# One group of 65536 keys a head in a decode attention kernel: scores in SBUF, one maximum, values in 32 KB rows

## The chip, the core and the metric

The kernel runs on one core of one Trainium2 chip. The core has a matrix engine (TensorE, PE in the profile), a vector engine (VectorE, DVE), a scalar engine (ScalarE, ACT), a general engine (GpSimd, POOL) and a synchronising engine (SyncE, SP), each with its own instruction queue that is worked through in order. Sixteen DMA engines move data from the chip's memory (HBM) to the on-chip memory SBUF, which has 128 partitions. PE writes its results to a second on-chip memory, PSUM. The metric is the device time of one execution in microseconds (us); lower is better.

## The reference

One token of a decoder, with two branches that are added:

```python
xn = _layernorm(x)
return x + _A_ref(xn, A_k_cache, A_v_cache, A_wq, A_wo) + _B_ref(xn, B_w1, B_w2, B_w3, B_w4)

def _A_ref(x, k_cache, v_cache, wq, wo):        # Hq = 32, Hkv = 4, Sk = 65536, Dh = 128, D = 1024
    q = (x @ wq) as [1, 32, 1, 128]
    k = repeat(k_cache, 8 times along the heads); v likewise
    scores = einsum("bhqd,bhkd->bhqk", q, k) * 128 ** -0.5
    p = softmax(scores)
    o = einsum("bhqk,bhkd->bhqd", p, v)
    return o as [1, 1, 4096] @ wo

def _B_ref(x, w1, w2, w3, w4):                  # one position: the shifts of the reference leave zeros here
    h = gelu(layernorm(x) @ w1); hs = concat(shifted parts of h) @ w2; x1 = x + hs
    return x1 + gelu(layernorm(x1) @ w3) @ w4
```

Everything is in bfloat16. Four key-value heads serve 8 query heads each. K and V are 67 MB each, the six weight matrices together some 36 MB: 170 MB are read once. A softmax needs the largest score before its exponentials (or a correction afterwards, when a larger one turns up).

## The kernel before, in words

The program is written with explicit queues. Every operation is appended to the list of its engine by a helper (`_op`, `_grp` for a group, `_dma`), which also adds waits on the semaphores of what it reads and overwrites. The order of the Python code is thus the order in each engine's queue.

**Slots and loads.** All large inputs pass through eight slots of SBUF, `slots_sb`, each of 16 KB a partition (8192 elements of 2 bytes). `load` (L290) fills one slot with 2 MB, `load2` (L296) two neighbouring slots with 4 MB in one transfer, and then needs an even slot number (`room`, L278). Slots are taken in a ring. All these transfers are issued on SP's queue. Lists `loads` and `uses` (L608 on) hold the order; after each use the function `issue` (L636) hands out as many further loads as have slots in the order of the list. On SP, a load waits until what was in its slots has been read. `wq` (8 MB, for the queries), `w1`, `w2` and `w3` come first, `w4` last, and a 2 MB part of `wo` a head in between.

**Groups.** The keys of a head are cut in two groups of 32768. A group has four chunks of 8192 keys (`NCH = 4`, 64 keys a partition). K of a group comes as two transfers of 4 MB: a partition's 256 keys of the group are 64 KB in HBM, of which each transfer takes 32 KB. V comes as four transfers of 2 MB, one a chunk, 16 KB a partition and without gaps. Chunks of K of group g alternate with chunks of V of group g-1.

**Scores.** `use_k` (L515) turns one chunk: four 32x32 block transposes by DVE (L522, 128x1024 in f32 units) from the slot to one of two buffers `X`, then 16 matrix products by PE (L529) into one of four PSUM banks `S_ps`, one bank a chunk, then DVE's maximum of the bank (L534). Eight query heads and sixteen key positions share the 128 PSUM partitions.

**Maximum and exponentials.** After four chunks `finish_group` (L536) takes the maximum over the chunks, brings it together over the partitions of a query head by one product (L543) and a minimum of the negated values, and updates a running maximum `brun` (L545 to L548). ACT then computes four exponentials from PSUM to `p_sb` with their sums (L553), and a correction factor `ff` for the second group (L557).

**Values.** `transpose_p` (L559) runs behind the first K chunk of the next group: eight PE transposes (L562) into PSUM and an ACT copy to `pT_sb` (L565), twice. `use_v` (L569) does 16 products a chunk (L575), summed in one PSUM bank `OT_ps`. `flash` (L580) copies the first group's result to `O_acc` (L585, ACT) and rescales and adds the second's (L588, L592, DVE). At a head's end `combine` (L594) sums the parts with five products (L595, L597) and four DVE steps (L600 to L604), which give the head's 1024 outputs for `use_wo`.

Of the kernel before, what the change touches and what calls it, by code (L numbers as in the profile page):

```python
# [133 lines left out]
def bass_parallel_sum__gqa_block_cached__mixer_s_mlp__decode_kernel(  # L134
# [23 lines left out]
    NCH = 4  # L158
    NA = 4
    SUB = P * CR  # L160
    GRP = SUB * NCH
    GPH = SK // GRP
    NG = HKV * GPH
    NK = NG * NCH
# [4 lines left out]
    assert DH == P and G == 8 and HKV == 4 and D == 1024 and HQD == 4096 and F == 3584 and SK % GRP == 0  # L169
# [5 lines left out]
    with ExitStack() as es:  # L175
# [42 lines left out]
        p_sb = sb("p_sb", [P, CL, 32, NCH], BF)  # L218
        pT_sb = sb("pT_sb", [P, 2, NA, CL * 4, G], BF)
        mcol = sb("mcol", [P, 2, NCH], F32)  # L220
        mrow = sb("mrow", [P, 2], F32)
        Rm = sb("Rm", [P, 2, 16], BF)
        Bst = sb("Bst", [P, NG], F32)
        brun = sb("brun", [P, 2], F32)
        dd = sb("dd", [P, 1], F32)
        ff = sb("ff", [P, 1], F32)
        lcol = sb("lcol", [P, 2, NCH], F32)
        lsum = sb("lsum", [P, 1], F32)
# [15 lines left out]

        S_all = ps("S_ps", [P, NCH * 512], F32)
        S_ps = [S_all[:, 512 * i:512 * (i + 1)] for i in range(NCH)]
# [110 lines left out]
        def load_v(g, a):
            h, gb = divmod(g, GPH)
            s0 = gb * GRP + a * SUB
            return load(A_v_cache[0, h, s0:s0 + SUB, :].rearrange("(p c) d -> p (c d)", p=P))  # L360

# [153 lines left out]
        def use_k(g, ch, ld):  # L515
            view, b = ld[0:2]
            n = g * NCH + ch
            h = g // GPH
            m = n % 2
            K32 = view.bitcast(F32)  # L520
            for ix in range(4):
                _op(q_dve, lambda e, ix=ix: e.transpose(out=X32[:, m, 1024 * ix:1024 * (ix + 1)], in_=K32[:, 1024 * ix:1024 * (ix + 1)]),  # L522
                    reads=b, writes=[b_X[m][ix]])
            fns = []
            for we in range(4):
                w_hi, e_ = divmod(we, 2)
# [7 lines left out]
            _op(q_dve, lambda e: e.reduce_max(mcol[:, gm, ch:ch + 1], S_ps[ch][:, :], axis=AX.X), reads=[b_S[ch]], writes=[b_mcol[gm]], partial=ch > 0)  # L534

        def finish_group(g):  # L536
            h, gb = divmod(g, GPH)
            m = g % 2
            kn, ko = gb % 2, (gb - 1) % 2
            _op(q_dve, lambda e: e.reduce_max(mrow[:, m:m + 1], mcol[:, m, :], axis=AX.X), reads=[b_mcol[m]], writes=[b_mrow[m]])  # L540
            _op(q_dve, lambda e: e.tensor_tensor(out=Rm[:, m, :], in0=sel16[:, :], in1=mrow[:, m:m + 1].broadcast_to([P, 16]), op=ALU.mult),
                reads=[b_mrow[m], b_const], writes=[b_R[m]])
            _op(q_pe, lambda e: e.matmul(M0_ps[:, 16:32], Lmat[:, :], Rm[:, m, :], start=True, stop=True), reads=[b_R[m], b_sel], writes=[b_M0])  # L543
            if gb == 0:
                _op(q_dve, lambda e: e.tensor_reduce(out=brun[:, 0:1], in_=M0_ps[:, 16:32], axis=AX.X, op=ALU.min), reads=[b_M0], writes=[b_brun[0]])  # L545
            else:
                _op(q_dve, lambda e: e.tensor_reduce(out=Bst[:, g:g + 1], in_=M0_ps[:, 16:32], axis=AX.X, op=ALU.min), reads=[b_M0], writes=[b_Bst])
                _op(q_dve, lambda e: e.tensor_tensor(out=brun[:, kn:kn + 1], in0=brun[:, ko:ko + 1], in1=Bst[:, g:g + 1], op=ALU.min),  # L548
                    reads=[b_brun[ko], b_Bst], writes=[b_brun[kn]])
                _op(q_dve, lambda e: e.tensor_tensor(out=dd[:, :], in0=brun[:, kn:kn + 1], in1=brun[:, ko:ko + 1], op=ALU.subtract),  # L550
                    reads=[b_brun[ko], b_brun[kn]], writes=[b_dd])
            for ch in range(NCH):
                _op(q_act, lambda e, ch=ch: e.activation(p_sb[:, :, :, ch], S_ps[ch][:, :].rearrange("p (c i) -> p c i", i=32),  # L553
                                                         ACTF.Exp, bias=brun[:, kn:kn + 1], scale=SCALE, accum_out=lcol[:, m, ch:ch + 1]),
                    reads=[b_S[ch], b_brun[kn]], writes=[b_p, b_lcol[m]], partial=ch > 0)
            if gb > 0:
                _op(q_act, lambda e: e.activation(ff[:, :], dd[:, :], ACTF.Exp), reads=[b_dd], writes=[b_ff])  # L557

        def transpose_p(g):  # L559
            m = g % 2  # L560
            for c8 in range(CL // 8):
                _grp(q_pe, [lambda e, i=i, c=8 * c8 + i: e.transpose(out=PT_ps[:, i * P:(i + 1) * P],  # L562
                                                                    in_=p_sb[:, c, :, :].rearrange("p i h -> p (i h)"), identity=ident_bf[:])
                            for i in range(8)], reads=[b_p, b_const], writes=[b_PT])
                _op(q_act, lambda e, c8=c8, m=m: e.activation(pT_sb[:, m, :, 32 * c8:32 * c8 + 32, :].rearrange("p a x g -> p x a g"),  # L565
                                                              PT_ps[:, :].rearrange("p (x a g) -> p x a g", x=32, a=NA), ACTF.Copy),
                    reads=[b_PT], writes=[b_pT[m]], partial=c8 > 0)

        def use_v(g, a, ld):  # L569
            view, b = ld[0:2]  # L570
            m = g % 2
            fns = []
            for cl in range(CL):
                q4 = cl % 4
                fns.append(lambda e, cl=cl, q4=q4: e.matmul(OT_ps[32 * q4:32 * q4 + 32, :], pT_sb[:, m, a, 4 * cl:4 * cl + 4, :].rearrange("p x g -> p (x g)"), view[:, 512 * cl:512 * (cl + 1)],  # L575
                                                            start=(a == 0 and cl < 4), stop=(a == NA - 1 and cl >= CL - 4), tile_position=(0, 32 * q4),
                                                            skip_group_check=True))
            _grp(q_pe, fns, reads=b + [b_pT[m]], writes=[b_OT], partial=a > 0)

        def flash(g):  # L580
            gb = g % GPH
            m = g % 2
            _op(q_dve, lambda e: e.reduce_sum(lsum[:, :], lcol[:, m, :], axis=AX.X), reads=[b_lcol[m]], writes=[b_lsum])
            if gb == 0:
                _op(q_act, lambda e: e.activation(O_acc[:, :], OT_ps[:, :], ACTF.Copy), reads=[b_OT], writes=[b_O])  # L585
                _op(q_dve, lambda e: e.tensor_copy(Lacc[:, :], lsum[:, :]), reads=[b_lsum], writes=[b_Lacc])
                return
            _op(q_dve, lambda e: e.tensor_scalar(out=O_acc[:, :], in0=O_acc[:, :], scalar1=ff[:, 0:1], scalar2=None, op0=ALU.mult),  # L588
                reads=[b_ff], writes=[b_O])
            _op(q_dve, lambda e: e.tensor_scalar(out=Lacc[:, :], in0=Lacc[:, :], scalar1=ff[:, 0:1], scalar2=lsum[:, 0:1], op0=ALU.mult, op1=ALU.add),  # L590
                reads=[b_ff, b_lsum], writes=[b_Lacc])
            _op(q_dve, lambda e: e.tensor_tensor(out=O_acc[:, :], in0=O_acc[:, :], in1=OT_ps[:, :], op=ALU.add), reads=[b_OT], writes=[b_O])  # L592
# [17 lines left out]
        for g in range(NG):  # L610
            for cp in range(2):
                loads.append(("k", g, cp))
                if g > 0:
# [101 lines left out]
```

## Time and profile before

| what | value |
|---|---|
| median of 3 runs | 406.20 us (406.18 to 406.21) |
| the profiled execution | 406.29 us |
| its span, first to last instruction | 404.6 us |
| mean granted TensorE clock | 0.615 |
| HBM read | 169.87 MB, 420 GB/s over the span |
| transposes of K (L522, DVE) | 128 times 1211 ns, 147.7 us |
| score products (L529, PE) | 512, 59.9 us busy |
| exponentials (L553, ACT) | 32 times 1412 ns, 45.2 us |
| value products (L575, PE) | 512, 55.9 us busy |

The page of the profile shows one execution. Busy times are sums over instructions; PE's matrix products overlap, so the busy time is less than count times mean. The rows of 40 slices give each engine's busy share in tenths, the clock that was granted to PE, and the share and rate of the sixteen DMA engines. The table of queues gives a DMA queue's packets, its MB, and the time that its packets took as a share of sixteen engines over the span. The chain of waits goes back from the last instruction to what released it, step by step. Timelines give the start of an instruction (or of a run of equal ones), its length, engine and line. The trace also holds each DMA packet with its start, length and size.

### The profile page before, as it was taken

Reading aid. Unit: us, or ns where it says so; the run is one execution under the profiler, and the core shown is the slowest. Engines: PE = TensorE matmul, PEld = TensorE weight load, DVE = VectorE, ACT = ScalarE, POOL = GpSimd, SP = SyncE. Lnnn points to the kernel's source line nnn. Section 1 sums busy time; section 2 is a strip of 40 time slices with the busy share of each in tenths; the row PEclk is TensorE's granted clock in tenths of the full one; section 3 lists DMA queues with packets and bytes.
Section 4 is the critical chain, followed back from the end, with each engine's and each line's share of the span. In section 5 each row is a group of like instructions: output and inputs, shape, how many; then the busy total and the mean of one; then the engine's idle time right before and its main releaser. Section 6 shows DMA issues by size and latency. Waiting matters only on the chain.

```text
span 404.6 us, 4047 instructions
## 1 busy us (share of the span) xinstructions
PE 170.8 (42%) x1651; PEld 75.4 (19%) x1651; DVE 200.4 (50%) x304; ACT 65.2 (16%) x91; POOL 7.5 (2%) x38
## 2 busy tenths in 40 slices
PE   0273231223555345435335363535252436355626
PEld 0122110102212112211121131212121122122313
DVE  0255027667667665755173737571545655740010
ACT  1000000006007105200610041106010232034000
POOL 5000000000000000000000000000000000000000
PEclk9985655555655965665556655656565657655656
DMA  8999999999999999999999999999999999999995
GB/s 357 421 415 426 452 415 444 413 437 420 462 400 431 429 447 411 441 414 444 411 450 410 437 424 441 415 427 439 423 433 434 423 434 424 420 434 420 444 405 197
DMA packets 9682, 170.13 MB, mean 421 GB/s; under 512 B 1208, under 2 KB 1216, under 8 KB 2112
## 3 DMA queue, kind: packets, MB, share of 16 engines
q1 hardware_dynamic: 9512, 169.88, 98.5%
q8 instruction: 13, 0.21, 0.2%
q14 instruction: 5, 0.04, 0.0%
q10 hardware_dynamic: 152, 0.00, 0.0%
HBM read 169.87 MB, written 0.00 MB: 420 GB/s over the span
## 4 chain that ended last, share of the span: by engine, by line
DMA 57%; DVE 21%; PE 13%; issue 6%; ACT 2%; SPq 0%; POOL 0%; ACTq 0%
DMA slots_sb<-in_A_k_cache_dram 47%; DVE X L522 17%; PE S_ps L529 8%; DMA slots_sb<-in_B_w_dram 7%; DMA xr_bf<-in_A_x_dram 3%; DVE mcol L534 3%; PE OT_ps L575 2%; PE S_ps L440 2%; ACT p_sb L553 1%; ACT pT_sb L565 1%; PE PT_ps L562 1%; PE M_ps L424 0%; PE M_ps L416 0%; PE M_ps L543 0%; SPq L317 0%
## 5 line engine op out<-in xcount | busy, mean ns | idle before, releaser
L522 DVE STREAM_TRANSPOSE X<-slots_sb 128x1024 f32<-128x1024 f32 x128 | 147.7, 1211 | 39.1 <-DMA slots_sb<-in_A_k_cache_dram 39.1
L529 PE MATMUL S_ps<-X,Yall 128*32 128x512 bf16 x512 | 59.9, 614 | 150.4 <-DVE X L522 150.4
L553 ACT ACTIVATE p_sb<-S_ps,brun 128x512 bf16<-128x512 f32 x32 | 45.2, 1412 | 195.5 <-DVE brun L545 105.2
L575 PE MATMUL OT_ps<-slots_sb,pT_sb 128*32 128x512 bf16 x512 | 55.9, 584 | 12.8 <-ACT pT_sb L565 9.6
L534 DVE TENSOR_REDUCE mcol<-S_ps 128x1 f32<-128x512 f32 x32 | 22.1, 692 | 69.2 <-PE S_ps L529 69.2
L529 PEld LDWEIGHTS S_ps<-X,Yall 128*32 128x32 bf16 x512 | 17.3, 126 | 185.8 <-DVE X L522 169.4
L575 PEld LDWEIGHTS OT_ps<-slots_sb,pT_sb 128*32 128x32 bf16 x512 | 18.5, 132 | 37.9 <-issue 32.2
L565 ACT ACTIVATE pT_sb<-PT_ps 128x1024 bf16<-128x1024 bf16 x16 | 16.4, 1023 | 55.6 <-PE PT_ps L562 55.6
L562 PE MATMUL PT_ps<-ident_bf,p_sb 128*128 128x128 bf16 x128 | 15.3, 294 | 11.8 <-ACT pT_sb L565 8.9
L440 PE MATMUL S_ps<-slots_sb,xn_bf 128*32 128x512 bf16 (+1 forms) x128 | 12.6, 567 | 10.7 <-DMA slots_sb<-in_B_w_dram 9.2
L562 PEld LDWEIGHTS PT_ps<-ident_bf,p_sb 128*128 128x128 bf16 x128 | 11.4, 133 | 20.3 <-ACT pT_sb L565 11.0
L592 DVE TENSOR_TENSOR O_acc<-O_acc,OT_ps 128x512 f32<-128x512 f32 x4 | 2.8, 688 | 16.5 <-PE OT_ps L575 16.5
L440 PE MATMUL M_ps<-slots_sb,gh_bf 128*32 128x256 bf16 x112 | 6.5, 399 | 7.7 <-DMA slots_sb<-in_B_w_dram 7.6
L444 DVE STREAM_TRANSPOSE X<-S_ps 128x512 f32<-128x512 f32 (+1 forms) x3 | 2.5, 848 | 14.2 <-PE S_ps L440 14.2
L452 ACT ACTIVATE ge_a<-ge_b 128x8 f32<-128x8 f32 (+1 forms) x2 | 0.4, 217 | 52.2 <-DVE ge_b L451 52.2
L678 DVE TENSOR_TENSOR fin<-accr,M_ps 128x256 bf16<-128x256 f32 x1 | 0.4, 421 | 16.3 <-PE M_ps L440 16.3
L553 ACT ACTIVATION_READ_ACCUMULATOR p_sb<-S_ps,brun 128x1 f32 x32 | 8.5, 264 | 0.0
L440 PE MATMUL M_ps<-slots_sb,oP_bf 128*32 128x256 bf16 x128 | 7.7, 420 | 1.4 <-DVE oP_bf L604 1.4
L597 PE MATMUL M_ps<-O_acc,selX 128*128 128x128 f32 x32 | 8.2, 439 | 0.0
L440 PEld LDWEIGHTS S_ps<-slots_sb,xn_bf 128*32 128x32 bf16 x128 | 4.3, 133 | 17.0 <-DMA slots_sb<-in_B_w_dram 9.9
L597 PEld LDWEIGHTS M_ps<-O_acc,selX 128*128 128x128 f32 x32 | 7.3, 333 | 0.0
L395 DVE CAST xP<-xP_bf 128x8 f32<-128x8 bf16 x1 | 0.2, 172 | 14.2 <-DMA xr_bf<-in_A_x_dram 14.2
(97 smaller groups left out, 70.1 us busy)
## 6 DMA issues: line engine op xcount, KB each, us to landing
slots_sb<-in_A_k_cache_dram SPq DMA_DIRECT2D x16, 4096.0 KB, 26.9
slots_sb<-in_A_v_cache_dram SPq DMA_DIRECT2D x32, 2048.0 KB, 30.7
slots_sb<-in_A_wq_dram SPq DMA_DIRECT2D x2, 4096.0 KB, 16.8
slots_sb<-in_A_wo_dram SPq DMA_DIRECT2D x4, 2048.0 KB, 27.5
slots_sb<-in_B_w_dram SPq DMA_DIRECT2D x2, 3584.0 KB, 33.5
slots_sb<-in_B_w_dram SPq DMA_DIRECT2D x2, 2048.0 KB, 28.1
slots_sb<-in_B_w_dram SPq DMA_DIRECT2D x1, 4096.0 KB, 31.9
slots_sb<-in_B_w_dram SPq DMA_DIRECT2D x5, 512.0 KB, 32.4
```

The costliest lines, as they stand in the source:

```text
L440: e.matmul(out_fn(j), st_fn(kk), mv_fn(kk, j), start=st, stop=sp, tile_position=(0, 32 * j), skip_group_check=True))
L444: _op(q_dve, lambda e: e.transpose(out=X32[:, 1, c0:c0 + 32 * n], in_=src), reads=b_src, writes=[b_X[1][0]], partial=c0 > 0)
L452: _op(q_act, lambda e: e.activation(a_, bb_, ACTF.Tanh, scale=math.sqrt(2.0 / math.pi)), reads=[b_ge], writes=[b_ge])
L522: _op(q_dve, lambda e, ix=ix: e.transpose(out=X32[:, m, 1024 * ix:1024 * (ix + 1)], in_=K32[:, 1024 * ix:1024 * (ix + 1)]), reads=b, write ...
L529: fns.append(lambda e, we=we, c_mid=c_mid, mv=mv: e.matmul(S_ps[ch][32 * c_mid:32 * c_mid + 32, :], Yall[:, h, we, :, :].rearrange("p a g ...
L534: _op(q_dve, lambda e: e.reduce_max(mcol[:, gm, ch:ch + 1], S_ps[ch][:, :], axis=AX.X), reads=[b_S[ch]], writes=[b_mcol[gm]], partial=ch > 0)
L553: _op(q_act, lambda e, ch=ch: e.activation(p_sb[:, :, :, ch], S_ps[ch][:, :].rearrange("p (c i) -> p c i", i=32), ACTF.Exp, bias=brun[:, k ...
L562: _grp(q_pe, [lambda e, i=i, c=8 * c8 + i: e.transpose(out=PT_ps[:, i * P:(i + 1) * P], in_=p_sb[:, c, :, :].rearrange("p i h -> p (i h)") ...
L565: _op(q_act, lambda e, c8=c8, m=m: e.activation(pT_sb[:, m, :, 32 * c8:32 * c8 + 32, :].rearrange("p a x g -> p x a g"), PT_ps[:, :].rearr ...
L575: fns.append(lambda e, cl=cl, q4=q4: e.matmul(OT_ps[32 * q4:32 * q4 + 32, :], pT_sb[:, m, a, 4 * cl:4 * cl + 4, :].rearrange("p x g -> p ( ...
L592: _op(q_dve, lambda e: e.tensor_tensor(out=O_acc[:, :], in0=O_acc[:, :], in1=OT_ps[:, :], op=ALU.add), reads=[b_OT], writes=[b_O])
L597: fns.append(lambda e, t=t: e.matmul(M0_ps[:, 256:384], selX[:, t, :, :].rearrange("p g x -> p (g x)"), O_acc[:, t * P:(t + 1) * P], start ...
```

## The change

The two groups of a head become one.

- `NCH` is 8: all of a head's 65536 keys are one group of eight chunks. The scores of a chunk still appear in one of four PSUM banks (chunk number modulo 4). ACT copies them from there to a new SBUF buffer `S_sb` (`max_k`), behind DVE's maximum of the bank. DVE's maximum of a chunk is placed behind the transposes of the next chunk.
- There is one maximum a head. The running maximum, the correction factor and `flash` are gone; `finish_head` computes four exponentials of 1024 elements from `S_sb`. `combine` copies `OT_ps` to `O_acc` by ACT, once a head.
- V is loaded by `load2`: four transfers of 4 MB a head, 32 KB a partition. For K, a partition holds 512 consecutive keys of the head, 128 KB, of which each of the four transfers takes 32 KB.
- The order of use becomes two chunks of K, then two of V. `transpose_p` has four rounds and stands behind the second K chunk. A head's part of `wo` is used two heads later, behind the first two V chunks; for the last heads at the end.

```diff
-    NCH = 4
+    NCH = SK // (P * CR)
...
+        S_sb = sb("S_sb", [P, NCH, 512], F32)
+        p_sb = sb("p_sb", [P, 2, CL, 32, NB], BF)
...
-        def load_k(g, cp):
-            h, gb = divmod(g, GPH)
-            v = A_k_cache[0, h, gb * GRP:(gb + 1) * GRP, :].rearrange("(p c) d -> p (c d)", p=P)
+        def load_k(h, cp):
+            v = A_k_cache[0, h, :, :].rearrange("(p c) d -> p (c d)", p=P)
             return load2(v[:, 2 * cp * SLOT:2 * (cp + 1) * SLOT])
...
+        def load_v(h, a):
+            n = SK // NA
+            return load2(A_v_cache[0, h, a * n:(a + 1) * n, :].rearrange("(p c) d -> p (c d)", p=P))
...
+            if ch > 0:
+                max_k(ch - 1)
...
+        def max_k(ch):
+            bank = ch % 4
+            _op(q_dve, lambda e: e.reduce_max(mcol[:, ch:ch + 1], S_ps[bank][:, :], axis=AX.X), reads=[b_S[bank]], writes=[b_mcol], partial=ch > 0)
+            _op(q_act, lambda e: e.activation(S_sb[:, ch, :], S_ps[bank][:, :], ACTF.Copy), reads=[b_S[bank], b_mcol], writes=[b_Ss[ch]])
+
+        def finish_head(h):
+            max_k(NCH - 1)
+            _op(q_dve, lambda e: e.reduce_max(mrow[:, 0:1], mcol[:, :], axis=AX.X), reads=[b_mcol], writes=[b_mrow])
...
+            for x in range(NB):
+                _op(q_act, lambda e, x=x: e.activation(p_sb[:, :, :, :, x], S_sb[:, 2 * x:2 * x + 2, :].rearrange("p s (c i) -> p s c i", i=32),
+                                                       ACTF.Exp, bias=brun[:, 0:1], scale=SCALE, accum_out=lcol[:, h % 2, x:x + 1]),
+                    reads=[b_Ss[2 * x], b_Ss[2 * x + 1], b_brun], writes=[b_p, b_lcol[h % 2]], partial=x > 0)
...
-        def flash(g):
...
         def combine(h):
+            _op(q_dve, lambda e: e.reduce_sum(Lacc[:, :], lcol[:, h % 2, :], axis=AX.X), reads=[b_lcol[h % 2]], writes=[b_Lacc])
+            _op(q_act, lambda e: e.activation(O_acc[:, :], OT_ps[:, :], ACTF.Copy), reads=[b_OT], writes=[b_O])
...
+        for h in range(HKV):
+            for i in range(4):
+                loads.append(("k", h, i))
+                uses += [("k", h, 2 * i), ("k", h, 2 * i + 1)]
+                if h > 0:
+                    loads.append(("v", h - 1, i))
+                    uses += [("v", h - 1, 2 * i), ("v", h - 1, 2 * i + 1)]
+                if h > 1 and i == 0:
+                    loads.append(("wo", h - 2))
+                    uses.append(("wo", h - 2))
+        for i in range(4):
+            loads.append(("v", HKV - 1, i))
+            uses += [("v", HKV - 1, 2 * i), ("v", HKV - 1, 2 * i + 1)]
+            if i == 0:
+                loads.append(("wo", HKV - 2))
+                uses.append(("wo", HKV - 2))
...
-        doubles = {"wq", "w3", "k"}
+        doubles = {"wq", "w3", "k", "v"}
...
-                if ch == 0 and g > 0:
-                    transpose_p(g - 1)
+                h, ch = args
+                use_k(h, ch, ld)
+                if ch == 1 and h > 0:
+                    transpose_p(h - 1)
                 if ch == NCH - 1:
-                    finish_group(g)
+                    finish_head(h)
```

More of the change, by code (lines that the diff above doesn't have):

```diff
@@ L157, in bass_parallel_sum__gqa_block_cached__mixer_s_mlp__decode_kernel @@
     CR = 64
-    NCH = 4
+    NCH = SK // (P * CR)
     NA = 4
[L160 to L164, printed above, removed]
+    NB = NCH // 2
     NT = F // P
@@ L168, in bass_parallel_sum__gqa_block_cached__mixer_s_mlp__decode_kernel @@
     FW = F // 4
-    assert DH == P and G == 8 and HKV == 4 and D == 1024 and HQD == 4096 and F == 3584 and SK % GRP == 0
+    assert DH == P and G == 8 and HKV == 4 and D == 1024 and HQD == 4096 and F == 3584 and SK == 65536
     SCALE = float(DH) ** -0.5
@@ L217, in bass_parallel_sum__gqa_block_cached__mixer_s_mlp__decode_kernel @@
         X = sb("X", [P, 2, SLOT], BF)
[L218 to L228, printed above, removed]
+        S_sb = sb("S_sb", [P, NCH, 512], F32)
+        p_sb = sb("p_sb", [P, 2, CL, 32, NB], BF)
+        pT_sb = sb("pT_sb", [P, NA, 2 * CL * 4, G], BF)
+        mcol = sb("mcol", [P, NCH], F32)
+        mrow = sb("mrow", [P, 1], F32)
+        Rm = sb("Rm", [P, 16], BF)
+        brun = sb("brun", [P, 1], F32)
+        lcol = sb("lcol", [P, 2, NB], F32)
         Lacc = sb("Lacc", [P, 1], F32)
@@ L243, in bass_parallel_sum__gqa_block_cached__mixer_s_mlp__decode_kernel @@
         fin = sb("fin", [P, RW], BF)
-        S_all = ps("S_ps", [P, NCH * 512], F32)
-        S_ps = [S_all[:, 512 * i:512 * (i + 1)] for i in range(NCH)]
+        S_all = ps("S_ps", [P, 4 * 512], F32)
+        S_ps = [S_all[:, 512 * i:512 * (i + 1)] for i in range(4)]
         PT_ps = ps("PT_ps", [P, 1024], BF)
@@ L263, in bass_parallel_sum__gqa_block_cached__mixer_s_mlp__decode_kernel @@
         b_X = [[_B() for _ in range(4)] for _ in range(2)]
-        b_S = [_B() for _ in range(NCH)]
+        b_S = [_B() for _ in range(4)]
+        b_Ss = [_B() for _ in range(NCH)]
         b_PT = _B()
         b_OT = _B(); b_M0 = _B(); b_M1 = _B()
-        b_mcol = [_B(), _B()]; b_mrow = [_B(), _B()]; b_R = [_B(), _B()]
-        b_Bst = _B(); b_brun = [_B(), _B()]; b_dd = _B(); b_ff = _B()
-        b_p = _B(); b_pT = [_B(), _B()]; b_lcol = [_B(), _B()]; b_lsum = _B(); b_Lacc = _B(); b_O = _B()
+        b_mcol = _B(); b_mrow = _B(); b_R = _B(); b_brun = _B()
+        b_p = _B(); b_pT = _B(); b_lcol = [_B(), _B()]; b_Lacc = _B(); b_O = _B()
         b_cb = _B(); b_oP = [_B() for _ in range(HKV)]
@@ L350, in load_w4 @@
             return [(view, [(bu, k0, k) for bu, (k0, k) in zip(bufs, at_)], i)]
-        def load_k(g, cp):
-            h, gb = divmod(g, GPH)
-            v = A_k_cache[0, h, gb * GRP:(gb + 1) * GRP, :].rearrange("(p c) d -> p (c d)", p=P)
+        def load_k(h, cp):
+            v = A_k_cache[0, h, :, :].rearrange("(p c) d -> p (c d)", p=P)
             return load2(v[:, 2 * cp * SLOT:2 * (cp + 1) * SLOT])
[L357 to L360, printed above, removed]
+        def load_v(h, a):
+            n = SK // NA
+            return load2(A_v_cache[0, h, a * n:(a + 1) * n, :].rearrange("(p c) d -> p (c d)", p=P))
         evs = []
@@ L511, in use_wo, with use_k @@
             rows_mv(R, d_parts(view, 0), lambda kk: oP_bf[:, h * R + kk:h * R + kk + 32], b_oP[h], b, [b_M1], False, False)
-        def use_k(g, ch, ld):
+        def use_k(h, ch, ld):
             view, b = ld[0:2]
-            n = g * NCH + ch
-            h = g // GPH
-            m = n % 2
+            m = ch % 2
+            bank = ch % 4
             K32 = view.bitcast(F32)
@@ L529, in use_k @@
                     fns.append(lambda e, we=we, c_mid=c_mid, mv=mv: e.matmul(
-                        S_ps[ch][32 * c_mid:32 * c_mid + 32, :], Yall[:, h, we, :, :].rearrange("p a g -> p (a g)"), mv,
+                        S_ps[bank][32 * c_mid:32 * c_mid + 32, :], Yall[:, h, we, :, :].rearrange("p a g -> p (a g)"), mv,
                         start=(we == 0), stop=(we == 3), tile_position=(0, 32 * c_mid)))
-            _grp(q_pe, fns, reads=b_X[m] + [b_Y], writes=[b_S[ch]])
-            gm = g % 2
@@ L534, in use_k @@
[L534 to L557, printed above, removed]
@@ L559, in transpose_p @@
-        def transpose_p(g):
-            m = g % 2
-            for c8 in range(CL // 8):
+            _grp(q_pe, fns, reads=b_X[m] + [b_Y], writes=[b_S[bank]])
+        def max_k(ch):
+            bank = ch % 4
+            _op(q_dve, lambda e: e.reduce_max(mcol[:, ch:ch + 1], S_ps[bank][:, :], axis=AX.X), reads=[b_S[bank]], writes=[b_mcol], partial=ch > 0)
+            _op(q_act, lambda e: e.activation(S_sb[:, ch, :], S_ps[bank][:, :], ACTF.Copy), reads=[b_S[bank], b_mcol], writes=[b_Ss[ch]])
@@ new lines, in finish_head @@
+        def finish_head(h):
+            max_k(NCH - 1)
+            _op(q_dve, lambda e: e.reduce_max(mrow[:, 0:1], mcol[:, :], axis=AX.X), reads=[b_mcol], writes=[b_mrow])
+            _op(q_dve, lambda e: e.tensor_tensor(out=Rm[:, :], in0=sel16[:, :], in1=mrow[:, 0:1].broadcast_to([P, 16]), op=ALU.mult),
+                reads=[b_mrow, b_const], writes=[b_R])
+            _op(q_pe, lambda e: e.matmul(M0_ps[:, 16:32], Lmat[:, :], Rm[:, :], start=True, stop=True), reads=[b_R, b_sel], writes=[b_M0])
+            _op(q_dve, lambda e: e.tensor_reduce(out=brun[:, 0:1], in_=M0_ps[:, 16:32], axis=AX.X, op=ALU.min), reads=[b_M0], writes=[b_brun])
+            for x in range(NB):
+                _op(q_act, lambda e, x=x: e.activation(p_sb[:, :, :, :, x], S_sb[:, 2 * x:2 * x + 2, :].rearrange("p s (c i) -> p s c i", i=32),
+                                                       ACTF.Exp, bias=brun[:, 0:1], scale=SCALE, accum_out=lcol[:, h % 2, x:x + 1]),
+                    reads=[b_Ss[2 * x], b_Ss[2 * x + 1], b_brun], writes=[b_p, b_lcol[h % 2]], partial=x > 0)
@@ L562, in transpose_p @@
+        def transpose_p(h):
+            for c8 in range(2 * CL // 8):
                 _grp(q_pe, [lambda e, i=i, c=8 * c8 + i: e.transpose(out=PT_ps[:, i * P:(i + 1) * P],
-                                                                    in_=p_sb[:, c, :, :].rearrange("p i h -> p (i h)"), identity=ident_bf[:])
+                                                                    in_=p_sb[:, c // CL, c % CL, :, :].rearrange("p i h -> p (i h)"), identity=ident_bf[:])
                             for i in range(8)], reads=[b_p, b_const], writes=[b_PT])
-                _op(q_act, lambda e, c8=c8, m=m: e.activation(pT_sb[:, m, :, 32 * c8:32 * c8 + 32, :].rearrange("p a x g -> p x a g"),
-                                                              PT_ps[:, :].rearrange("p (x a g) -> p x a g", x=32, a=NA), ACTF.Copy),
-                    reads=[b_PT], writes=[b_pT[m]], partial=c8 > 0)
@@ L569, in use_v @@
-        def use_v(g, a, ld):
+                _op(q_act, lambda e, c8=c8: e.activation(pT_sb[:, :, 32 * c8:32 * c8 + 32, :].rearrange("p a x g -> p x a g"),
+                                                         PT_ps[:, :].rearrange("p (x a g) -> p x a g", x=32, a=NA), ACTF.Copy),
+                    reads=[b_PT], writes=[b_pT], partial=c8 > 0)
+        def use_v(h, n, ld):
             view, b = ld[0:2]
-            m = g % 2
+            a, lo = divmod(n, 2)
             fns = []
@@ L574, in use_v @@
                 q4 = cl % 4
[L575 to L578, printed above, removed]
@@ L580, in flash @@
-        def flash(g):
[L581 to L592, printed above, removed]
+                x0 = 4 * (CL * lo + cl)
@@ new lines, in use_v @@
+                fns.append(lambda e, cl=cl, q4=q4, x0=x0: e.matmul(OT_ps[32 * q4:32 * q4 + 32, :], pT_sb[:, a, x0:x0 + 4, :].rearrange("p x g -> p (x g)"), view[:, 512 * cl:512 * (cl + 1)],
+                                                                   start=(n == 0 and cl < 4), stop=(n == 2 * NA - 1 and cl >= CL - 4), tile_position=(0, 32 * q4),
+                                                                   skip_group_check=True))
+            _grp(q_pe, fns, reads=b + [b_pT], writes=[b_OT], partial=n > 0)
@@ L609, in bass_parallel_sum__gqa_block_cached__mixer_s_mlp__decode_kernel @@
         uses = [("wq", j) for j in range(4)] + [("w1",), ("w2",)] + [("w3", j) for j in range(4)]
[L610 to L613, printed above, removed]
-                    loads += [("v", g - 1, 2 * cp), ("v", g - 1, 2 * cp + 1)]
-            for ch in range(NCH):
-                uses.append(("k", g, ch))
-                if g > 0:
-                    uses.append(("v", g - 1, ch))
-            if g > GPH and g % GPH == 1:
-                h = g // GPH - 1
-                loads.append(("wo", h))
-                uses.append(("wo", h))
-        loads += [("v", NG - 1, a) for a in range(NA)] + [("wo", HKV - 1)] + [("w4", i) for i in (0, 2, 3)]
-        uses += [("v", NG - 1, a) for a in range(NA)] + [("wo", HKV - 1)] + [("w4", i) for i in range(4)]
+        for h in range(HKV):
[14 more added lines that the diff above has]
+                uses.append(("wo", HKV - 2))
+        loads += [("wo", HKV - 1)] + [("w4", i) for i in (0, 2, 3)]
+        uses += [("wo", HKV - 1)] + [("w4", i) for i in range(4)]
         layer_norm(xP, b_x, xn, xn_bf, b_xn, 0)
@@ L656, in bass_parallel_sum__gqa_block_cached__mixer_s_mlp__decode_kernel @@
             elif kind == "k":
-                g, ch = args
-                use_k(g, ch, ld)
-                if ch == 0 and g > 0:
-                    transpose_p(g - 1)
+                h, ch = args
+                use_k(h, ch, ld)
+                if ch == 1 and h > 0:
+                    transpose_p(h - 1)
                 if ch == NCH - 1:
-                    finish_group(g)
+                    finish_head(h)
             elif kind == "v":
-                g, a = args
-                if g == NG - 1 and a == 0:
-                    transpose_p(g)
-                use_v(g, a, ld)
-                if a == NA - 1:
-                    flash(g)
-                    if g % GPH == GPH - 1:
-                        combine(g // GPH)
+                h, n = args
+                if h == HKV - 1 and n == 0:
+                    transpose_p(h)
+                use_v(h, n, ld)
+                if n == 2 * NA - 1:
+                    combine(h)
             else:
```

## The prediction, made before the result was known

> **What bounds the kernel now.** I read the page first: the span, the busy shares, the slices, and the table of DMA queues; its last line here is the chain of waits by engine.
>
> ```profile
> span 404.6 us, 4047 instructions
> ...
> PE 170.8 (42%) x1651; PEld 75.4 (19%) x1651; DVE 200.4 (50%) x304; ACT 65.2 (16%) x91; POOL 7.5 (2%) x38
> ...
> DMA  8999999999999999999999999999999999999995
> ...
> q1 hardware_dynamic: 9512, 169.88, 98.5%
> ...
> DMA 57%; DVE 21%; PE 13%; issue 6%; ACT 2%; SPq 0%; POOL 0%; ACTq 0%
> ```
>
> No engine is busy for more than half of the span, while the sixteen DMA engines are occupied for 98.5% of it. Then the stretches of 20 us (columns: PE, PEld, DVE, ACT, POOL busy, clock, DMA share, GB/s):
>
> ```profile
> 5.00:25.00 20.00, 7.20 (x57) 3.25 (x57) 4.33 (x21) 0.00 (x0) 2.33 (x11) 1.00 1.00 428
> 85.00:105.00 20.00, 9.32 (x81) 4.10 (x85) 12.97 (x15) 7.67 (x10) 0.00 (x0) 0.50 1.00 429
> ...
> 285.00:305.00 20.00, 8.93 (x80) 4.01 (x80) 10.54 (x10) 2.05 (x2) 0.00 (x0) 0.59 1.01 429
> ```
>
> The rate is the same in the opening, where only wq is moving, and in the attention, so compute does not hold it back. The trace's packet records say the same: first data packet at 2.11 us, last at 401.5, so a stream of 399.4 us; the packets' times, summed and divided by 16, are 398.5 (queue q1) and 1.2 (the others). The stream has no holes. That chain names DVE and PE too (21% and 13%), but only as the work that frees a slot for a transfer that then joins a queue; an issue lands a median 26.9 us (K) and 30.7 us (V) later, that is, behind some three 4 MB transfers. So the time is 2.1 us to the first packet, the stream, and 3.1 us to the end. An edit counts if it shortens the packets or if it lets the queue run empty.
>
> **The packets.** The same records give, by size: 16384 B, median 613 ns, mean 616.5; 32768 B, median 1215, mean 1221.6. V moves today as 32 transfers of 128 packets of 16 KB, 4096/16 = 256 packets an engine; after the change as 16 transfers, 128 packets of 32 KB an engine. By means: 256 x 0.6165 = 157.8 us against 128 x 1.2216 = 156.4: -1.45. Each transfer also ends with a 4-byte packet of 9 ns on every engine; 16 fewer: -0.14. K keeps its 2048 packets of 32 KB, but the address step from one partition to the next doubles, from 64 KB to 128 KB. In this trace the step does not show: wq alone (64 KB step) has median 1213, packets among K 1213 to 1215, and V, whose partitions follow each other without a gap, 613 for its 16 KB. I take 0. From above: the slowest bytes of any packet from 4 KB up are the 4096-byte ones (162 ns, 25.3 B/ns against 27.0), which would make 32 KB last 1296 ns, 81 x 128 = +10.4 us; from below nothing, as every large packet is already at 26.7 to 27.0 B/ns.
>
> **Work that moves beside the stream.** ACT gets 32 copies of scores from PSUM (128x512 f32, the form of L585: 0.59 us, 18.9 in all), and 16 Exp of 1024 elements for 32 of 512. The Exp rows:
>
> ```profile
> 90.77 1.40 ACT L553 ACTIVATE p_sb<-S_ps,brun 128x512 bf16<-128x512 f32 x1 [34.52 <-DVE brun L545]
> 91.90 0.26 ACT L553 ACTIVATION_READ_ACCUMULATOR p_sb<-S_ps,brun 128x1 f32 x1
> 92.26 1.39 ACT L553 ACTIVATE p_sb<-S_ps,brun 128x512 bf16<-128x512 f32 x1
> ```
>
> One takes 1.49 from start to start, the accumulator is read 1.13 after the start, and the one-element Exp (L557) takes 0.21. So (1.13-0.21)/512 = 1.8 ns an element, and the long one 1.49 + 512 x 1.8 ns = 2.41. Lower end: 1.93 (plain copies: 1.023 for 1024, 0.588 for 512, +0.44); upper: 2.98 (twice). I take 2.41, since the output's step of 8 bytes and the accumulation stay. ACT then has 8 x 0.59 + 4 x 2.41 + 4 x 1.02 + 0.59 = 19 us a head, within some 78 us of transfers: hidden. By the Trainium skill, "ScalarE: Activation LUTs", section "What ACT_TABLE_LOAD costs", an ACTIVATE with a pointer as bias takes about 280 ns and 0.833 ns an element, so 1.13 us for 1024; the trace has that at 512 already, so the trace decides, and with the page's figure only the margin below would grow.
>
> DVE keeps its 128 transposes and 32 maxima. The maximum of a chunk now stands behind the next chunk's transposes, so DVE no longer waits 2.09 us on PE each time (7.31 us a chunk today, 4.62 + 0.61 = 5.23 then). L588, L592 and the running-maximum steps go. It is off the path in both: worth 0. SP issues 16 transfers fewer, 0.33 us each, beside the stream. POOL's queue is untouched.
>
> **Where the queue could run dry.** Every load now takes a pair of the eight slots, and a wo load, which takes one, makes the next pair skip the other. So a load waits for the one four places ahead of it to be used. The tight place is the end of heads 1 and 2. The loads there run: last K pair of head h, V(h-1,3), K(h+1,0), V(h,0), wo(h-1), K(h+1,1), V(h,1), K(h+1,2); the last needs the slots of V(h,0). Let DVE start on the last K pair at 0:
> - Transposes, a maximum, transposes: 4.62 + 0.61 + 4.60 = 9.83.
> - Scores, last maximum, row maximum, M0 product, brun, start of Exp: 3.74 (87.03 to 90.77 in the trace): 13.57.
> - Four Exp, 4 x 2.41: 23.2.
> - New in ACT's order: O_acc of head h-1 is copied behind these Exp, 0.59: 23.8. PE's combine products and DVE's four combine steps wait for that, with DVE's next transposes queued behind them (DVE idle some 13 us). They take 3.83 (381.92 to 385.75 at the end of the trace): 27.7.
> - Transposes of K(h+1,0): 9.17, then scores of its second chunk 2.05: 38.9.
> - Four rounds of eight p transposes and a copy, now behind the second K chunk where they stood behind the first. Two took 97.28 to 101.68, four then 8.70: 47.6.
> - 32 value products (48 took 5.27): 3.55: 51.15. V(h,0) is free.
> - SP's issue: 0.05, and 1.33 to the first packet (0.78 to 2.11 at the start): 52.5.
>
> On the other side, the last K packet ended 0.42 before DVE's start (60.04 and 60.46 for the first K pair). Five pairs follow, 8 x 1.2216 = 9.77 each, and wo, 8 x 0.6165 = 4.93: the queue lasts until 5 x 9.77 + 4.93 - 0.42 = 53.4. The margin is 0.9 us, so no stall. With the short Exp it is 2.8; with the long one 4 x 0.57 = 2.3 later, a stall of 1.4 at each of two heads, +2.8. That is what I take for the bounds of this term: 0 to +2.8, taken 0.
>
> Elsewhere the margin is wider. Behind head 0 there is no wo and no combine. In the last head V(3,3) needs V(3,0): PE's combine ends at 26.5, p transposes 8.7, products 3.55, issue 1.4: 40.1, and the queue lasts for four pairs and wo, 4 x 9.77 + 4.93 - 0.42 = 43.6. Behind V(3,3), products, copy and combine (3.55 + 0.59 + 3.83 = 8 us) lie beside wo(3) and w4, 4.9 and 17 us of transfers. The end is the same w4 pieces.
>
> **The sum.** -1.45 - 0.14 + 0 + 0 = -1.6 us against the profiled execution: 406.29 with a span of 404.6; its 0.1 above the median of 406.2 is the spread of the runs. 406.2 - 1.6 = 404.6.
>
> **Rivals.**
> - *The queue runs dry* at heads 1 and 2, through an Exp nearer twice the short one or other waits in that chain. For it: a margin of only 0.9 us, and ACT's new order puts the copy of O_acc behind four Exp. Against: the chain is summed from the trace's own gaps. It decides from an Exp of 2.63 us on. Full price +2.8: 407.4. Small stalls, 0.4 to 1.2 a head, would end as no change, about 406.0.
> - *K's packets get slower* with the 128 KB step. This is the one that ends on the other side most clearly: it makes the kernel slower from a mean K packet of 1240 ns on (1.6 + 0.8 = 2.4 us over 128 packets, 18 ns). Against it: no dependence from 16 to 64 KB. With half of the bound above, 41 ns a packet, +5.2 - 1.6: 409.8. The Trainium skill, "DMA: Bandwidth & Descriptors", section "Latency and other measured facts", speaks against the change here: rows of 16 KiB at a step of 512 KiB moved at 207 GB/s where a padded step gave 214, and less at larger steps. That is 3.3%, an estimate of +5.2 us on K if 128 KB were already as bad; no run here shows a step of 128 KB yet.
> - *The larger packet saves nothing* because the port, not the packet, is the limit: 406.2. Against it: the fixed 9 to 12 ns between two halves and a whole is in 4877 and 2432 packets.
>
> **The chances.** No stall, 404.6: 0.58. Small stalls or no saving, 405.4 to 407.0: 0.20. Full stalls, 407.1 to 407.4 and beyond, or another wait: 0.12. Slow K packets: 0.10. A measurement of this kernel can tell about 0.2%, 0.8 us, from no change: faster 0.58, same 0.20, slower 0.22. Low end: a saving of 2.0, since the mean 16 KB packet varies by a few ns from stretch to stretch: 404.2. High end: the full stall, 407.4; slow K packets stay outside.
>
> **What would show it.** Right: q1 with 9512 - 2048 - 256 = 7208 packets, the same share of time in it, DMA at 9 in every slice, and SP's waits for freed slots ending before the queue is empty. DVE should show an idle of about 13 us at each head's end, on PE's combine, without a price. Wrong: a slice below 9 near the third and fourth head's start (the queue ran dry), or full slices with fewer GB/s (slow packets).

## The result, and the profile after

The changed kernel takes 408.95 us (median of 5, 408.29 to 409.36) against 406.20 for the kernel before: a ratio of 1.0064 (95% interval 1.0053 to 1.0075). It is slower by 2.75 us, where 1.6 us less was forecast, and outside the range of 404.2 to 407.4. The profiled execution was the slowest of the five, 409.36 us.

The page of the changed kernel, the lines that answer to those of before:

```profile
span 407.4 us, 3981 instructions
...
DMA  8999999999999999999999999999999999999994
...
q1 hardware_dynamic: 7208, 169.87, 97.7%
...
DMA 68%; DVE 21%; PE 7%; issue 3%; SPq 1%; POOL 0%; ACTq 0%
```

The packets are the 7208 that were worked out. At first sight the DMA engines are as busy as before: every slice but the first and the last shows a 9, because a 9 means 90% or more of 10 us. But q1's share has dropped from 98.5% to 97.7%. Shorter stretches show where. Columns as in the prediction (engines busy, clock, DMA share, GB/s); first the kernel before, then the changed one:

```profile
205.00:215.00 10.00, 5.43 (x48) 2.77 (x52) 7.21 (x7) 2.05 (x2) 0.00 (x0) 0.50 1.04 447
285.00:300.00 15.00, 7.53 (x68) 3.65 (x72) 9.84 (x9) 2.05 (x2) 0.00 (x0) 0.50 1.03 440
360.00:375.00 15.00, 9.80 (x105) 4.98 (x109) 1.54 (x8) 8.15 (x12) 0.00 (x0) 0.50 1.01 429
```

```profile
205.00:215.00 10.00, 8.43 (x128) 4.27 (x128) 7.22 (x8) 1.28 (x3) 0.00 (x0) 0.80 0.94 392
285.00:300.00 15.00, 10.52 (x144) 5.97 (x144) 10.42 (x10) 3.83 (x5) 0.00 (x0) 0.69 0.88 364
360.00:375.00 15.00, 9.11 (x136) 4.64 (x136) 0.00 (x0) 1.40 (x2) 0.00 (x0) 0.80 0.94 380
```

In these three stretches, and in no other before the end, the sixteen DMA engines are not all at work. They are the starts of heads 2 and 3 and the middle of the last head's values, and in each of them a load waits for the slots of V(h,0). By the packet records the engines' idle time there is 0.66, 1.37 and 0.57 us (mean over the sixteen); the trace of before has none.

One of these places in order of time, from the timeline (start, length, engine, line, and in brackets the idle time before with what ended it). DVE began the transposes of head 2's last K pair at 241.90. Some rows in between are left out:

```profile
241.90 4.62 DVE L512 STREAM_TRANSPOSE X<-slots_sb 128x1024 f32<-128x1024 f32 x4 [9.13 <-DMA slots_sb<-in_A_k_cache_dram]
...
255.49 2.70 ACT L539 ACTIVATE p_sb<-S_sb,brun 128x1024 bf16<-128x1024 f32 x1 [0.27 <-DVE Lacc L565]
...
258.31 2.57 ACT L539 ACTIVATE p_sb<-S_sb,brun 128x1024 bf16<-128x1024 f32 x1
...
265.88 0.63 ACT L566 ACTIVATE O_acc<-OT_ps 128x512 f32<-128x512 f32 x1
...
269.16 0.17 DVE L572 RECIPROCAL cb_rL<-M_ps 128x1 f32<-128x1 f32 x1 [13.70 <-PE M_ps L569]
...
270.24 9.12 DVE L512 STREAM_TRANSPOSE X<-slots_sb 128x1024 f32<-128x1024 f32 x8
...
290.03 3.60 PE L559 MATMUL OT_ps<-slots_sb,pT_sb 128*32 128x512 bf16 x32 [1.21 <-ACT pT_sb L548]
...
293.73 0.33 SPq L295 DMA_DIRECT2D slots_sb<-in_A_k_cache_dram  x1
```

The reader sees the chain that was summed in the prediction, with its 13.7 us of idle DVE, and at its end the load of K(3,2), issued at 293.73. Its first packet starts at 294.70. Each transfer ends with a 4-byte packet on each engine; here are the ends of the first, the middle and the last of these sixteen, from the packet records of the changed kernel (us, on the timeline's zero; "last to last" is the step from the last one of the transfer before):

```
transfer     first    middle   last     last to last
K(3,1)       283.26   283.56   285.21
V(2,1)       292.99   293.27   294.93    9.72
K(3,2)       304.82   305.18   306.33   11.40
```

Most engines had nothing left from 293.0 to 293.5 on, and stood still for at least 1.2 to 1.7 us. At the other two places the same step (last to last) is 11.00 and 10.65, where undisturbed ones take 9.71. The three excesses, 1.29 + 1.69 + 0.94, are 3.9 us.

### The profile page after: what moved, and what is told of

It is laid out like the page before. It is cut to its first block, busy times and chain, and to the rows that moved or that the text cites. A ratio compares the mean times of both kernels' runs of the same rounds, so it can differ in the third digit from the quotient of the medians.

```text
span 407.4 us, 3981 instructions
## 1 busy us (share of the span) xinstructions
PE 156.6 (38%) x1647; PEld 71.8 (18%) x1647; DVE 187.8 (46%) x264; ACT 80.5 (20%) x87; POOL 7.5 (2%) x38
## 3 DMA queue, kind: packets, MB, share of 16 engines
q1 hardware_dynamic: 7208, 169.87, 97.7%
## 4 chain that ended last, share of the span: by engine, by line
DMA 68%; DVE 21%; PE 7%; issue 3%; SPq 1%; POOL 0%; ACTq 0%
DMA slots_sb<-in_A_k_cache_dram 51%; DVE X L512 18%; DMA slots_sb<-in_B_w_dram 7%; DMA slots_sb<-in_A_v_cache_dram 7%; DMA xr_bf<-in_A_x_dram 3%; PE OT_ps L559 3%; DVE mcol L528 2%; PE S_ps L431 2%; PE S_ps L521 1%; SPq L310 1%; PE M_ps L407 0%; PE M_ps L415 0%; PE M_ps L536 0%; POOL ln_s L419 0%; DVE Rm L534 0%
## 5 line engine op out<-in xcount | busy, mean ns | idle before, releaser
L521 PE MATMUL S_ps<-X,Yall 128*32 128x512 bf16 x512 | 56.1, 582 | 147.2 <-DVE X L512 147.2
L529 ACT ACTIVATE S_sb<-S_ps 128x512 f32<-128x512 f32 x32 | 19.2, 599 | 206.9 <-DVE mcol L528 206.9
L559 PE MATMUL OT_ps<-slots_sb,pT_sb 128*32 128x512 bf16 x512 | 47.3, 533 | 16.2 <-DMA slots_sb<-in_A_v_cache_dram 11.4
L521 PEld LDWEIGHTS S_ps<-X,Yall 128*32 128x32 bf16 x512 | 16.4, 121 | 181.9 <-DVE X L512 167.0
L539 ACT ACTIVATE p_sb<-S_sb,brun 128x1024 bf16<-128x1024 f32 x16 | 41.6, 2597 | 1.9 <-DVE Lacc L565 0.8
L528 DVE TENSOR_REDUCE mcol<-S_ps 128x1 f32<-128x512 f32 x32 | 21.1, 658 | 7.1 <-PE S_ps L521 7.1
L548 ACT ACTIVATE pT_sb<-PT_ps 128x1024 bf16<-128x1024 bf16 x16 | 16.4, 1024 | 19.2 <-PE PT_ps L545 19.2
L545 PE MATMUL PT_ps<-ident_bf,p_sb 128*128 128x128 bf16 x128 | 14.1, 277 | 13.4 <-ACT pT_sb L548 13.4
L567 PE MATMUL M_ps<-Lacc,selL 128*128 128x1 f32 x8 | 2.2, 348 | 24.6 <-ACT O_acc L566 24.6
L566 ACT ACTIVATE O_acc<-OT_ps 128x512 f32<-128x512 f32 x4 | 2.5, 619 | 23.3 <-PE OT_ps L559 23.3
```

Source lines behind the costliest of these rows:

```text
L521: fns.append(lambda e, we=we, c_mid=c_mid, mv=mv: e.matmul(S_ps[bank][32 * c_mid:32 * c_mid + 32, :], Yall[:, h, we, :, :].rearrange("p a ...
L528: _op(q_dve, lambda e: e.reduce_max(mcol[:, ch:ch + 1], S_ps[bank][:, :], axis=AX.X), reads=[b_S[bank]], writes=[b_mcol], partial=ch > 0)
L529: _op(q_act, lambda e: e.activation(S_sb[:, ch, :], S_ps[bank][:, :], ACTF.Copy), reads=[b_S[bank], b_mcol], writes=[b_Ss[ch]])
L539: _op(q_act, lambda e, x=x: e.activation(p_sb[:, :, :, :, x], S_sb[:, 2 * x:2 * x + 2, :].rearrange("p s (c i) -> p s c i", i=32), ACTF.Ex ...
L548: _op(q_act, lambda e, c8=c8: e.activation(pT_sb[:, :, 32 * c8:32 * c8 + 32, :].rearrange("p a x g -> p x a g"), PT_ps[:, :].rearrange("p ...
L559: fns.append(lambda e, cl=cl, q4=q4, x0=x0: e.matmul(OT_ps[32 * q4:32 * q4 + 32, :], pT_sb[:, a, x0:x0 + 4, :].rearrange("p x g -> p (x g) ...
```

## The experiments

Two explanations stood against each other. **A**: the queue ran dry in these three places, since the slots of V(h,0) came free too late; the packets themselves are as cheap as forecast. **B**: the new address step of K, or the long rows of V, or the coarser slots, cost time by themselves, and the idle spots are a by-product. The first four kernels ran side by side with the kernel before (406.30 us in these runs), the last three again so (406.31).

### The copy of O_acc on DVE

```diff
-            _op(q_act, lambda e: e.activation(O_acc[:, :], OT_ps[:, :], ACTF.Copy), reads=[b_OT], writes=[b_O])
+            _op(q_dve, lambda e: e.tensor_copy(O_acc[:, :], OT_ps[:, :]), reads=[b_OT], writes=[b_O])
```

> The changed kernel with one edit: the copy of OT_ps to O_acc at a head's end is made by DVE instead of ACT, so that it no longer stands behind the four Exp of the next head. Theory A (the queue runs dry because the slots of V(h,0) come free too late, at the starts of heads 2 and 3 and once in the last head): the chain to V(h,0) gets shorter by what the copy waited, about 7 us at heads 2 and 3 (then the p transposes wait for DVE's K transposes, some 30 us after the start instead of 38) and 3 us in the last head; no slice has idle DMA engines before the end, and the time is 406.2 - 1.6 = 404.6 us (404.2 to 405.2). Theory B (K's 128 KB step or the 32 KB rows of V make packets slower): 408.5 to 409.4, as the changed kernel.

Measured: 405.20 us, ratio to the kernel before 0.9971 (0.9961 to 0.9982). It is faster than both kernels, by one line. The same three stretches and the timeline of head 2's end:

```profile
205.00:215.00 10.00, 4.89 (x48) 1.81 (x52) 7.43 (x8) 1.20 (x2) 0.00 (x0) 0.59 0.99 426
285.00:300.00 15.00, 7.64 (x92) 3.03 (x84) 10.02 (x10) 1.20 (x2) 0.00 (x0) 0.65 0.99 425
360.00:375.00 15.00, 6.91 (x108) 2.96 (x100) 0.00 (x0) 0.00 (x0) 0.00 (x0) 0.73 1.00 427
```

```profile
240.98 4.62 DVE L512 STREAM_TRANSPOSE X<-slots_sb 128x1024 f32<-128x1024 f32 x4 [9.12 <-DMA slots_sb<-in_A_k_cache_dram]
...
257.85 0.69 DVE L566 COPY O_acc<-OT_ps 128x512 f32<-128x512 f32 x1 [3.31 <-PE OT_ps L559]
...
261.16 9.12 DVE L512 STREAM_TRANSPOSE X<-slots_sb 128x1024 f32<-128x1024 f32 x8
...
281.07 3.60 PE L559 MATMUL OT_ps<-slots_sb,pT_sb 128*32 128x512 bf16 x32 [1.21 <-ACT pT_sb L548]
...
284.77 0.33 SPq L295 DMA_DIRECT2D slots_sb<-in_A_k_cache_dram  x1
```

The copy now takes place while ACT is in its second Exp. DVE starts the next K pair 20.2 us after the last one (28.3 before), and the load that waited for V(h,0) is issued at 43.8 instead of 51.8. The dry spells are gone (0.02 us of idle in all). That is A. The time sits at the upper edge of what was expected, 1.1 us saved instead of 1.6.

### The weight part wo later in the queue

```diff
-                if h > 1 and i == 0:
+                if h > 1 and i == 2:
...
-            if i == 0:
+            if i == 2:
                 loads.append(("wo", HKV - 2))
```

> The changed kernel with one edit: the load and the use of a part of wo stand behind the third pair of V chunks of a head instead of the first (in the last head too). Theory A: the queue behind V(h,0) then holds three 4 MB transfers instead of two and wo's 2 MB, so it lasts 4.8 us longer while the chain to V(h,0) is untouched (DVE stays idle 13.7 us a head's end); no dry spell, 404.6 us (404.2 to 405.2). Theory B: 408.5 to 409.4.

Measured: 405.48 us, ratio 0.9982 (0.9973 to 0.9990). Here nothing in the chain was shortened; only the queue behind V(h,0) was made 4.8 us longer, and the two spells at the heads' starts are gone as well. The median is 0.3 above the range that was expected. In the last head the edit does not lengthen the queue, which the expectation had missed: wo still lies among the three transfers behind V(3,0), now last of them instead of first, and 0.40 us of idle remains there:

```profile
285.00:300.00 15.00, 8.69 (x109) 4.25 (x106) 4.92 (x5) 3.13 (x4) 0.00 (x0) 0.73 0.99 425
360.00:375.00 15.00, 8.15 (x128) 3.95 (x128) 0.00 (x0) 0.32 (x1) 0.00 (x0) 0.73 0.98 405
```

### K's address step alone

In the kernel before:

```diff
-            v = A_k_cache[0, h, gb * GRP:(gb + 1) * GRP, :].rearrange("(p c) d -> p (c d)", p=P)
-            return load2(v[:, 2 * cp * SLOT:2 * (cp + 1) * SLOT])
+            v = A_k_cache[0, h, :, :].rearrange("(p c) d -> p (c d)", p=P)
+            return load2(v[:, (4 * gb + 2 * cp) * SLOT:(4 * gb + 2 * cp + 2) * SLOT])
```

> The kernel before with one part of the change: K's transfers read with 128 KB from partition to partition (each partition's keys of a group come from a head-wide row), all else as before. The keys of K then no longer belong to the values they are paired with, so the attention is computed on other pairs of keys and values; the work is the same. Theory A: the step costs nothing, packets of 32 KB keep their median of 1215 ns, 406.2 us (405.9 to 406.5). Theory B: over 408.

Measured: 406.29 us beside 406.30, ratio 1.0001 (0.9992 to 1.0009). The 2432 packets of 32 KB have the same median (1215 ns) and mean (1221.6) as before. A step of 128 KB costs nothing.

### The rows of V alone

In the kernel before, with the lists of loads changed to match:

```diff
-            s0 = gb * GRP + a * SUB
-            return load(A_v_cache[0, h, s0:s0 + SUB, :].rearrange("(p c) d -> p (c d)", p=P))
+            s0 = gb * GRP + 2 * cp * SUB
+            return load2(A_v_cache[0, h, s0:s0 + 2 * SUB, :].rearrange("(p c) d -> p (c d)", p=P))
...
-        doubles = {"wq", "w3", "k"}
+        doubles = {"wq", "w3", "k", "v"}
```

> The kernel before with one part of the change: V comes in transfers of 4 MB with 32 KB a partition, two chunks in one, all else as before (groups of 32768 keys, maximum from PSUM). The values then stand at other places than the weights expect, so the output is that of other pairs; the work is the same. Theory A: the packets save 1.6 us and the slots come free in time, since a group has only two rounds of p transposes and four short Exp: 404.6 us (404.2 to 405.2). Theory B, or a loss by the coarser slots alone: 406.5 or more.

Measured: 405.06 us, ratio 0.9970 (0.9958 to 0.9981). So the rows of V are what the change gains, and pairs of slots alone do no harm:

```profile
span 403.4 us, 4017 instructions
...
DMA  8999999999999999999999999999999999999995
...
q1 hardware_dynamic: 7208, 169.87, 98.4%
```

The gain is 1.24 us. The packets' times, summed over q1 and divided by 16, fall by 1.7 us (398.5 to 396.8), the end of the stream only by 1.3 (401.2 to 399.9). The difference lies in the records: on an engine a packet starts 3 to 4 ns before the end of the one before it, so the sum counts that much twice at every packet. An engine has 144 packets fewer now (594.5 and 450.5 on average), which is some 0.5 us of the 1.7. Counted from completion to completion, two transfers of V mostly took 9.79 us before and one of the double size takes 9.71: 0.08 us, 16 times, about what was gained.

### Two Exp more, in the changed kernel

```diff
-            for x in range(NB):
+            for j, x in enumerate([0, 1, 2, 3, 0, 1]):
...
-                    reads=[b_Ss[2 * x], b_Ss[2 * x + 1], b_brun], writes=[b_p, b_lcol[h % 2]], partial=x > 0)
+                    reads=[b_Ss[2 * x], b_Ss[2 * x + 1], b_brun], writes=[b_p, b_lcol[h % 2]], partial=j > 0)
```

> The changed kernel with two of the four Exp of a head done a second time (same inputs, same results), 2 x 2.6 = 5.2 us more on ACT behind each head's maximum; ACT as a whole has room (80 of 407 us busy). Theory A: everything behind the Exp in the chain to V(h,0) comes 5.2 us later, at the starts of heads 2 and 3 and in the last head, and since the queue runs dry there already, each of the three dry spells grows by 5.2: 3 x 5.2 = +15.6 over the changed kernel, 421 to 426 us. If the dry spells only happened to stand beside the loss: 409 to 410.

Measured: 423.77 us, ratio 1.0432 (1.0417 to 1.0448), as A said. 20.3 us of additional work (100.8 against 80.5) on an engine that had been busy for a fifth of the span cost about 15 us: three of the four heads paid for nearly all of their share.

```profile
PE 158.3 (38%) x1647; PEld 74.2 (18%) x1647; DVE 188.1 (45%) x264; ACT 100.8 (24%) x103; POOL 7.6 (2%) x38
```

The packet records add a detail. At heads 2 and 3 the delay appears in two spells, 1.9 us before the load that waits for K(h+1,0), and 3.7 to 3.8 us before the one that waits for V(h,0); in the last head in one of 4.3.

### Two Exp more, with the copy on DVE

> The same two extra Exp, in the kernel whose copy of OT_ps to O_acc is on DVE. Theory A: at heads 2 and 3 the p transposes wait there for DVE's transposes of K (about 31 us after the start), and six Exp end at 29.5, so nothing is late: no price. In the last head the p transposes wait for the Exp alone: V(3,0) comes free at about 42 and its successor's first packet at 43.2, against a queue that lasts until 42 on most engines: 0 to 1.2 us. Together 405.2 to 406.4 us. If ACT's time itself counts: as much more as in the other run, over 415.

Measured: 407.43 us, ratio 1.0027 (1.0017 to 1.0038): 2.2 us more than without the two Exp, where 15 had been paid above. The starts of heads 2 and 3 are as expected free of charge. The last head cost more than the 0 to 1.2 that was expected, and the time lies 1.0 above the expected range:

```profile
205.00:215.00 10.00, 4.93 (x48) 1.88 (x52) 7.40 (x8) 1.19 (x2) 0.00 (x0) 0.53 0.98 423
285.00:300.00 15.00, 7.87 (x104) 3.57 (x96) 10.01 (x10) 1.19 (x2) 0.00 (x0) 0.69 0.98 421
360.00:375.00 15.00, 9.07 (x136) 4.73 (x136) 0.00 (x0) 1.16 (x2) 0.00 (x0) 0.73 0.90 361
```

V(3,0) came free 41.7 us after DVE's start, as reckoned, and its successor's first packet came at 43.1; the mean idle is 1.7 us, and the packets' times are 0.75 us longer (397.33 against 396.58 in the sum over q1 divided by 16), which the expectation had left out.

### Copy on DVE and wo later

Both edits of the first two experiments together.

> Both edits, the copy on DVE and wo behind the third V pair. Theory A: the first edit alone already leaves no dry spell, so the second has nothing to remove: 405.2 us (405.0 to 405.4), as with the first alone. If the place of wo has a price of its own: 404.4 to 404.9.

Measured: 405.23 us, ratio 0.9975 (0.9964 to 0.9985), the same as with the copy alone. The place of wo has no price of its own; it mattered only through the length of the queue.

## Why the prediction was wrong

- *What bounds the kernel*: right. The time followed the DMA stream in every run, and ACT's or DVE's work cost only where it made the queue run dry.
- *The packets of V*: right in kind, too large in size. Forecast -1.6 us; with V's rows alone -1.24, with the copy on DVE -1.1. The sum added up the lengths of packets, which overlap by 3 to 4 ns; with 144 fewer of them it takes off some 0.5 us that was never spent. The two means were not clean either: 616.5 holds 13 packets of the instruction queue q8 (1059 ns on average), and 1221.6 the kernel's slow first packets. From 50 to 386 us, q1 alone, they are 615.6 and 1218.1, and the term would have been -1.68 instead of -1.45.
- *K's step*: right, worth 0. The run with the step alone is the first here that shows a step of 128 KB by itself, and its packets are unchanged, so nothing of this rival's 5.2 us came. For 512 KB nothing was run.
- *The long Exp*: 2.41 us from start to start were taken; the trace has about 2.6 (starts at 258.31, 260.92, 263.51), and 2.8 for the first. Four of them end with O_acc's copy starting at 265.88, that is 10.4 after the first, not 9.64. This is 0.75 us of the margin, within the bounds that were given.
- *The chain to V(h,0)*: nearly right. Its end was forecast 51.15 us after DVE's start; at head 2's end it was 51.7 (241.90 to 293.63).
- *How long the queue lasts*: **this is the step that failed.** It was reckoned from the landing of the K pair, "0.42 before DVE's start", thus for the last of the sixteen engines, and for that one it was nearly right: 53.4 forecast, 53.0 measured (294.93 - 241.90). But the middle engine had ended that K pair at 239.82, 2.1 us before DVE's start, and had its last packet done at 293.27, 51.4 after the start. The skew was there to be read in the trace of before: the sixteen completions of the first K pair lie at 58.53 (first), 58.69 (middle, 1.8 before DVE's start at 60.46) and 59.94 (last), and late in that trace the last is 1.7 behind the middle. The first packet of the next load came at 294.70, 52.8. So the margin of 0.9 us was 0.2 for the last engine and minus 1.4 for the middle one.
- *Two readings in that sum*: the prediction set the packet records 0.3 us late against the timeline (the first data packet starts at 1.81, not 2.11) and took 60.04 for the end of the first K pair, where the last completion is at 59.94. The way from SP's issue to the first packet is then 1.0 us instead of 1.33 (0.78 to 1.81; 293.73 to 294.70 in the changed kernel). Both together are 0.2 us of the margin, to its favour.
- *The price of a dry spell*: it was put at the missing time alone. The traces show a second part. The first packets of the load that ends a spell are slow: at 294.7 they last 1.3 to 2.1 us on all sixteen engines, instead of 1.2. In all, 90 packets of 32 KB last longer than 1.3 us in the changed kernel and 29 with the copy on DVE. Between these two kernels the packets' times differ by 1.4 us (397.97 and 396.58 in the sum over q1 divided by 16), the idle time by 2.6; together 4.0, and the streams end 3.85 us apart. Therefore the named rival, *the queue runs dry*, came true at three places instead of two and at 3.9 us instead of 2.8: -1.2 + 3.9 = +2.7.
- *The last head*: forecast free with a margin of 3.5 us; it paid 0.94. DVE began the last K pair here at 327.64:

```profile
327.64 4.62 DVE L512 STREAM_TRANSPOSE X<-slots_sb 128x1024 f32<-128x1024 f32 x4 [10.68 <-DMA slots_sb<-in_A_k_cache_dram]
```

  The chain was right: the first packet of V(3,3) came at 367.98, 40.3 after the start, 40.1 forecast. The queue was 43.3 long for the last engine, 43.6 forecast, but 40.6 for the middle one (368.23). That leaves the middle engine 0.3, and no loss by the skew alone. Seven engines in fact began V(3,3) within 0.01 us of their last packet; their first packets took 1.4 to 1.9 us all the same. Two began it only at 369.2 and 369.4, and ten packets were slow again from 370.7 to 371.2, without an idle spell before them. Why is open.

Shown by runs: that the loss is the dry queue, that it goes away by shortening the chain or by lengthening the queue, and that K's step and V's rows are innocent. That the queue was empty for most engines, and not for the last, is read from the completions in the records; no run changed the skew. The packets carry no engine's number, so it is only argued which engine lags. Followed back from packet to packet, the last completion of K(3,2) leads to a packet that starts at 295.79, and it and the next one last 1.63 us each. If that is the engine that ended V(2,1) last, at 294.93, its 1.69 us are 0.86 of idle time and 0.84 of slow packets. What makes the engines drift apart, and what makes first packets slow, stays open.

## What to carry to other kernels

In a kernel that is bound by its transfers, reckon the time from a slot's landing to its release against the time that the queue lasts, and do it for the engines that are ahead, not for the one whose completion opens the wait; a margin of less than the skew of the sixteen engines, here 1.7 us and more, is none. Do not add up the lengths of packets that overlap; take the step from completion to completion. Look at what stands ahead in each engine's queue: here a copy of 0.6 us behind four Exp made the vector engine idle for 13.7 us and cost 3.8 us, and that was gone once the idle engine made the copy. A long row of 9s in the slices does not prove a full queue: look at stretches of 10 us where loads wait for slots.

## What the runs showed of the hardware

- When a load reaches engines whose queue has run empty, its first 32 KB packets are slow: 1.3 to 2.1 us on all sixteen engines at 294.7 in the changed kernel and 1.7 to 2.3 in the last head with two more Exp, instead of 1.22; at the start of the kernel before, 1.2 to 2.1. An engine need not have stood still for it (last head, above). The price of a short dry spell was 1.3 to 1.5 times the mean idle time (2.2 us for 1.7, 4.0 for 2.6).
- The sixteen engines do not end a transfer together. In the kernel before, the last completion of a transfer of K or V lies 0.5 to 1.7 us behind the middle one, in the changed kernel up to 2.7.
- On one engine packets follow each other with 3 to 4 ns of overlap, so the sum of their lengths can exceed the time that passes.
- An Exp of 128x1024 with its sum, from SBUF in f32 to bf16 at a step of 8 bytes, took 2.57 us, and 2.6 from start to start (2.7 for the first one at the ends of heads 1 and 2). A copy of 128x1024 from PSUM (bf16) took 1.02.
- Packets of 32 KB have the same median of 1215 ns at 64 KB and at 128 KB from partition to partition.
